# The order of seven outer products in a fast matrix multiplication, and where two weight sums are made

## The chip, the cores and the metric

The kernel runs on one core of a Trainium2 chip. A core has a matrix engine (TensorE, PE in the profile), a vector engine (VectorE, DVE), an activation engine (ScalarE, ACT), a general engine (GpSimd, POOL) and a queue that mostly issues transfers (SyncE, SP). Each works through its own queue in order; semaphores tie the queues together. The metric is the device time of one execution in microseconds (us).

## The reference

The input is four batches of eight heads with 768 rows of 64 numbers. First comes routed attention, then a feed-forward block:

```python
mask = q_assign[:, :, :, None] == k_assign[:, :, None, :]   # nearest of 16 centroids
scores = np.where(mask, scale * np.matmul(q, k.transpose(0, 1, 3, 2)), -1e9)
attn_out = np.matmul(softmax(scores), v)
x = attn_out.transpose(0, 2, 1, 3).reshape(3072, 512)
h = x @ w_in                                  # w_in: 512 x 2048
g = h * (1.0 / (1.0 + np.exp(-1.702 * h)))    # quick Gelu
out = g @ w_out                               # w_out: 2048 x 512
```

All of it is in 32-bit floating point. The feed-forward block is done batch by batch, 768 rows at a time.

## The kernel before

The first part (to 346 us of the profiled span) is attention for all four batches, and the change does not touch it. Then come, for each batch b = 0 to 3, a first layer (72 us) and a second layer (64 us).

**First layer.** It multiplies with seven products of half-size blocks instead of eight (the Winograd form of Strassen's method). A loop over eight columns f makes seven products each on PE (first7, matmuls at L840). VectorE adds them up from PSUM (add, L831), ScalarE copies one and applies the Gelu (L845, L850), and the result lies in the tile G as four blocks. GpSimd makes the sums of w_in for the column after the next (sums_w, 128x256 operations at L593). VectorE follows with after7, which prepares operands of the second layer: G's signs, and from column 4 on one slice per column of the operands of the first outer product (tiles Y[11], E[0], E[1], E[2]).

**Second layer.** It applies the same method twice, so that 49 quarter-size products are made. The outer level has seven outer products, in the order of ORDER; k counts them, and i is the number of the product in the method. second49(k) makes one of them: seven inner products of four matmuls each (L890), in the order 1, 2, 6, 5, 7, 3, 4, accumulated in three PSUM banks x, z, v out of a pool of six. Inner products 1, 2 and 3 read G itself; 6, 5, 7 and 4 read sums of G (t2, t1, t3, t4; sums_t, 128x768 operations on VectorE); 6, 5 and 3 need sums of the weights from the tile W[k] (name Wz, two buffers), and the others read the weights. ScalarE copies from PSUM (L900 to L925), VectorE adds, and the outer product is left in a tile y of 128x768. For i = 1 the tile is Y[22] itself. Then the finished y is added into the quarters Y[11], Y[12], Y[21], Y[22] of the output that need it, on GpSimd (L593, Y<-y,Y), in the last batch for two of the products on VectorE. Product i = 4 comes last and is added into Y[21] piece by piece.

Between these, extra(at) puts other work of VectorE at three places of each outer product: the sums sums_t for the next outer product, sums_G (four operations that turn a block of G in place into the operand of a later outer product), the transposes of a finished quarter with its stores (store, L945 and L949), and the sums of x for the next batch.

**The weight sums.** In batch 0 alone they are made from w_out: three 128x512 operations on GpSimd per outer product (keep_w), into parts of Y[12], Y[21] and Y[22], each then stored to kept_w in main memory (L775). All seven sets are made in columns 3 to 7 of the first layer of batch 0, before which VectorE turns signs in w_out and its sums (turn_w). All batches load them back, three transfers per outer product (load_sums, L782), two outer products ahead.

**The end.** In the last batch the quarter Y[11] is stored from the fifth outer product on, the others in the last one (tail). Stores of the last quarter are cut into pieces and alternate between the queues of SyncE and ScalarE; the others are four transfers each on SyncE. A transfer waits for the one that was issued eight places before it.

Of the kernel before, what the change touches and what calls it, by code (L numbers as in the profile page):

```python
# [38 lines left out]
def fast(  # L39
# [26 lines left out]
    nc = tc.nc  # L66
# [676 lines left out]
                      (Sz(1, f), Sz(2, f), "+", Bz(0, 0, f)),  # L743
                      (Sz(4, f), Bz(1, 0, f), "-", Sz(2, f))))

    ORDER = (1, 7, 3, 2, 6, 5, 4)

    def W_of(i):

# [12 lines left out]
        a = W_of(i)  # L762
        sums(nc.vector, ((a(0, 1), a(0, 0), "-", a(0, 1)),))

    def keep_w(k):

        a = W_of(ORDER[k])
        s2, s1, s4 = (Y[n].rearrange("p a t -> p (a t)")[
            :, 0:FQ * P].rearrange("p (f n) -> p f n", n=P)
            for n in (12, 21, 22))  # L770
        for i, (o, x, op, z) in enumerate((
                (s2, a(1, 1), "-", a(0, 1)), (s1, s2, "+", a(0, 0)),
                (s4, a(1, 0), "-", s2))):
            sums(nc.gpsimd, ((o, x, op, z),))
            nc.sync.dma_start(out=kept_w[k, i], in_=o)  # L775

    W = {}

    def load_sums(k):
        W[k] = ws.tile([P, 3, FQ, P], FP32, name="Wz")  # L780
        for i in range(3):
            nc.sync.dma_start(out=W[k][:, i], in_=kept_w[k, i])  # L782

# [7 lines left out]
    def tile_x(i):  # L791
        return T_of[i].rearrange("p c (q t) -> p (c q) t", t=QT)

    def tile_y(n):
        return Y[n].rearrange("p m (q t) -> p (m q) t", t=QT)

    def temps(k):

        return dict(zip((3, 2, 1, 4), (
            (tile_y(11), E[0], E[1], E[2]),  # L800
            (tile_y(12), tile_x(2), tile_x(3), tile_x(4)),
            (tile_y(11), E[0], E[1], E[2]),
            (tile_x(2), tile_x(3), tile_x(4), E[0]),
            (E[1], E[2], tile_x(4), E[0]),
            (G_of(5)(0, 1), tile_x(2), E[1], E[2]),
            (G_of(4)(0, 1), E[0], E[1], E[2]))[k]))

    def sums_t(k, fs=slice(0, FQ)):
# [67 lines left out]
    def second49(k, extra, last):  # L876

        i = ORDER[k]
        a, g, t, w = W_of(i), G_of(i), temps(k), W.pop(k)
        A = {1: a(0, 0), 2: a(1, 0), 3: w[:, 2], 4: a(1, 1), 5: w[:, 1],  # L880
             6: w[:, 0], 7: a(0, 1)}
        M = {1: g(0, 0), 2: g(1, 0), 3: g(1, 1), 4: t[4], 5: t[1], 6: t[2],
             7: t[3]}

        def bank_b():
            return ps_b.tile([P, 512], FP32, name="b")[:, 0:QT]

        def product(ps, n, start):
            for f in range(FQ):
                nc.tensor.matmul(out=ps, lhsT=A[n][:, f], rhs=M[n][:, f],  # L890
                                 start=start and f == 0,
                                 stop=(f == FQ - 1), skip_group_check=True)

        y = Y[22] if i == 1 else ep.tile([P, 2, HALF], FP32, name="y")
        y11, y12, y21, y22 = (y[:, m, q * QT:(q + 1) * QT]
                              for m in range(2) for q in range(2))
        p5 = ep.tile([P, QT], FP32, name="p5")
        x = bank_b()
        product(x, 1, True)
        nc.scalar.copy(y11, x)  # L900
        z = bank_b()
        product(z, 2, True)
        add(y11, z, y11)
        extra(0)
        product(x, 6, False)
        nc.scalar.copy(y12, x)
        v = bank_b()
        product(v, 5, True)
        nc.scalar.copy(p5, v)
        product(x, 7, False)  # L910
        nc.scalar.copy(y22, x)
        add(y22, y22, p5)
        extra(1)
        product(v, 3, False)
        add(y12, v, y12)
        if i == 4:
            c = Y[21]
            add(c[:, 0], y[:, 0], c[:, 0])
            add(c[:, 1, QT:], y22, c[:, 1, QT:])
            extra(2)  # L920
        product(x, 4, False)
        if i == 4:
            add(c[:, 1, 0:QT], x, c[:, 1, 0:QT])
            return
        nc.scalar.copy(y21, x)  # L925
        extra(2)
        pool = nc.vector if last and i in (6, 5) else nc.gpsimd
        sums(pool, {1: (), 7: ((Y[21], y, "+", Y[22]),),
                    3: ((Y[12], y, "+", Y[22]),),
                    2: ((Y[11], y, "+", Y[22]),),  # L930
                    6: ((Y[12], y, "+", Y[12]), (Y[21], y, "+", Y[21])),
                    5: ((Y[12], y, "+", Y[12]), (Y[22], y, "+", Y[21]))}[i])

    def store(b, n, m=slice(0, 2), q=slice(0, 2), queues=(nc.sync,)):

        h, t = divmod(n, 10)
        h, t = h - 1, t - 1
        o = {11: T_of[3], 12: E[0], 22: E[1], 21: E[2]} if b < B - 1 else {
            11: T_of[3], 12: T_of[3], 22: T_of[4], 21: T_of[2]}
        o = o[n].rearrange("p a t -> p (a t)").rearrange(  # L940
            "p (j m i) -> p j m i", m=2, i=SQ)
        at, to = q.start * QT, q.stop * QT
        o = o[:, at // SQ:to // SQ]
        for one in range(m.start, m.stop):
            nc.vector.transpose(out=o[:, :, one], in_=Y[n][:, one, at:to])  # L945
        rows = out[b * S + t * HALF + at:b * S + t * HALF + to]
        for r in range(P // SQ):
            col = r * P + (2 * h + m.start) * SQ
            queues[r % len(queues)].dma_start(  # L949
                out=rows[:, col:col + (m.stop - m.start) * SQ].rearrange(  # L950
                    "(j t) i -> t j i", t=SQ),
                in_=o[r * SQ:(r + 1) * SQ, :, m].rearrange(
                    "t j m i -> t j (m i)"))
# [26 lines left out]
    for b in range(B):  # L980
        for f in range(FB):
            first7(b, f, *XT)
            sums_w(b * FB + f + 2)
            if f:
                after7(f - 1)
            do(pend, 1)
            if b == 0 and f < 3:
                for n in range(3 * f, min(3 * f + 3, FB)):
                    sums_z((nc.gpsimd, nc.vector, nc.vector)[n % 3], n)
            if b == 0 and f in (3, 4):  # L990
                for i in ORDER[0:4] if f == 3 else ORDER[4:]:
                    turn_w(i)
            if b == 0 and f >= 3:
                for k in {3: (0,), 4: (1, 2), 5: (3,), 6: (4, 5),
                          7: (6,)}[f]:
                    keep_w(k)
                if 5 <= f < 7:
                    load_sums(f - 5)
        after7(FB - 1)
        if b < B - 1:  # L1000
            for h in range(2):
                for hp in range(HP):
                    x = xT_of[b + 1, h, hp] = xp.tile([P, HALF], FP32,
                                                      name="x")
                    nc.sync.dma_start(out=x, in_=kept[b, h, hp])
            made = sums_x(b + 1)
        else:
            made = iter(())

        def stores(b, *todo, **how):  # L1010
            for n in todo:
                store(b, n, **how)
                yield

        both = dict(queues=(nc.sync, nc.scalar))

        def tail():
            for n in (12, 22):
                store(b, n)
                yield  # L1020
            store(b, 21, slice(0, 1), slice(0, 1), **both)
            store(b, 21, q=slice(1, 2), **both)
            yield

        def chain(*todo):
            for steps in todo:
                yield from steps

        def sums_of_x():
            for XT[:] in made:  # L1030
                yield

        x_steps = sums_of_x()
        final = b == B - 1

        for k in range(7):
            nxt = sums_t(k + 1) if k < 6 else iter(())
            more = {1: sums_G(6), 3: sums_G(5),
                    4: chain(sums_G(4), stores(b, 11)), 5: x_steps,
                    6: tail() if final else x_steps}.get(k, iter(()))  # L1040
            if b == B - 1 and k < 2:
                test(k)
            if (b, k) == (B - 1, 6):
                is_bad = nc.values_load(bad[0:1, 0:1], min_val=0, max_val=1)

            def extra(at):
                do(nxt, (2, 1, 1)[at])
                do(more, ((1, 1, 1) if final else (0, 4, 4))[at] if k == 6
                   else (0, 2, 2 + (k == 4))[at])

            second49(k, extra, final)
            if k < 5:
                load_sums(k + 2)
            elif b < B - 1:
                load_sums(k - 5)
        pend = () if final else stores(b, 12, 22, 21)
        if final:
            store(b, 21, slice(1, 2), slice(0, 1), **both)
# [439 lines left out]
```

## Time and profile before

| | us |
|---|---|
| median of three runs (920.73 to 921.88) | 921.24 |
| the profiled execution's own time | 914.16 |
| its span, first to last instruction | 912.4 |
| first layer of batch 0 | 346.6 to 418.9 |
| second layer of batch 0 | 418.9 to 491.7 |
| second layers of batches 1, 2, 3 | 564.0 to 628.0, 700.0 to 764.0, 836.4 to 900.5 |
| after the last matmul | 900.5 to 912.4 |

Busy shares of the span are PE 97%, VectorE 78%, GpSimd 53% and ScalarE 40%. PE is the engine whose idle time counts. A line of the page's slices gives the busy tenths of 40 equal parts of the span. A line of the waits names who waited, for whom, and then microseconds in total, times, and the longest. A line of the timeline gives start, length, engine, line of the code, operation, output and input tiles and shapes, the number of instructions taken together, and in brackets the idle time ahead of it. A line of the windows gives the stretch, its length, the busy time of the five engines, the granted clock, the share of the transfer engines and GB/s.

### The profile page before, as it was taken

To read this page: it belongs to the slowest core of one execution; us is meant where nothing else is said; L and a number is where in the kernel's file an instruction comes from. 1 tells how busy PE (TensorE), PEld (TensorE's weight loads), DVE (VectorE), ACT (ScalarE), POOL (GpSimd) and SP (SyncE) were. 2 spreads that over 40 slices of the span, in tenths; PEclk is the share of its full clock that TensorE was granted. 3 is DMA by queue.
4 is the path that set the end of the run, shared out by engine and by line. 5 is a ranking of instruction groups with operands and counts; after the bars stand their busy time and mean duration, and the time that the engine had idled before them with its cause. 6 is when DMAs were issued, how large, how long until landed. Compare 5 with 4: busy or idle time off the path is not lost.

```text
span 912.4 us, 17739 instructions
## 1 busy us (share of the span) xinstructions
PE 888.9 (97%) x6712; PEld 580.8 (64%) x6712; DVE 712.0 (78%) x1170; ACT 363.2 (40%) x816; POOL 481.1 (53%) x465
## 2 busy tenths in 40 slices
PE   8999999999999999997999999999999999999994
PEld 3444444444444445555998556998557997557994
DVE  4999999998899996998788556788556787556794
ACT  3767767776667773221111232112232112232110
POOL 5899899989999898696134121133121133220110
PEclk9999999999999999998999999999999999999998
DMA  9475556666574210037214202213202313200314
GB/s 184 118 125 102 101 118 144 143 128 136 127 135 111 84 43 18 9 129 243 84 56 122 52 1 70 84 57 120 52 1 70 97 50 115 52 1 1 104 46 97
DMA packets 179261, 80.55 MB, mean 88 GB/s; under 512 B 155368, under 2 KB 161632, under 8 KB 179168
## 3 DMA queue, kind: packets, MB, share of 16 engines
q1 hardware_dynamic: 177776, 79.11, 35.7%
q8 instruction: 55, 0.90, 0.4%
q10 hardware_dynamic: 1392, 0.23, 0.2%
q14 instruction: 38, 0.31, 0.1%
HBM read 62.61 MB, written 16.70 MB: 87 GB/s over the span
## 4 chain that ended last, share of the span: by engine, by line
PE 82%; DVE 5%; POOL 4%; DMA 3%; issue 2%; SPq 2%; ACT 2%; ACTq 0%; DVEq 0%; POOLq 0%
PE b L840 28%; PE b L890 28%; PE s L467 11%; PE o L532 9%; POOL Y L593 3%; PE m L549 2%; PE s L490 2%; ACT A L498 1%; DMA raw<-in_moe_w_out_dram 1%; SPq L418 1%; PE m L343 1%; DMA raw<-in_moe_w_in_dram 1%; POOL W L593 1%; DMA line<-row 1%; DVE x L570 1%
## 5 line engine op out<-in xcount | busy, mean ns | idle before, releaser
L516 POOL TENSOR_TENSOR sum<-sum,A 128x384 f32<-128x384 f32 x252 | 264.0, 1082 | 35.3 <-ACT A L498 22.1
L831 DVE TENSOR_TENSOR G<-b,G 128x384 f32<-128x384 f32 x224 | 123.1, 557 | 100.8 <-PE b L840 90.7
L498 ACT ACTIVATE A<-s 128x768 f32<-128x768 f32 x192 | 144.7, 804 | 94.0 <-PE s L490 73.8
L593 POOL TENSOR_TENSOR Y<-y,Y 128x768 f32<-128x768 f32 x24 | 59.4, 2483 | 186.8 <-DVE y L831 162.9
L467 PE MATMUL s<-T,T 64*64 64x384 f32 x1536 | 144.6, 491 | 2.6 <-ACT A L498 0.9
L845 ACT ACTIVATE G<-G 128x384 f32<-128x384 f32 x128 | 66.3, 523 | 198.1 <-DVE G L831 196.8
L532 PE MATMUL o<-A,inv 64*64 64x384 f32 x1536 | 141.5, 483 | 0.0
L593 POOL TENSOR_TENSOR W<-w_in 128x256 f32<-128x256 f32 x32 | 23.5, 735 | 164.5 <-PE b L840 164.2
L467 PEld LDWEIGHTS s<-T,T 64*64 64x64 f32 x1536 | 52.3, 132 | 78.6 <-ACT A L498 51.5
L840 PE MATMUL b<-x,W 128*128 128x384 f32 x256 | 93.0, 486 | 0.0
L840 PE MATMUL b<-Tx,w_in 128*128 128x384 f32 x256 | 93.0, 486 | 0.0
L840 PE MATMUL b<-x,w_in 128*128 128x384 f32 x256 | 88.5, 486 | 0.0
L593 DVE TENSOR_TENSOR G<-G 128x768 f32<-128x768 f32 (+1 forms) x88 | 84.3, 980 | 0.0
L532 PEld LDWEIGHTS o<-A,inv 64*64 64x64 f32 x1536 | 59.4, 133 | 37.6 <-issue 32.6
L840 PEld LDWEIGHTS b<-x,W 128*128 128x128 f32 x256 | 48.6, 190 | 33.9
L840 PEld LDWEIGHTS b<-Tx,w_in 128*128 128x128 f32 x256 | 48.6, 190 | 33.9
L840 PEld LDWEIGHTS b<-x,w_in 128*128 128x128 f32 x256 | 48.5, 190 | 33.5 <-issue 0.6
L890 PE MATMUL b<-E,Wz 128*128 128x192 f32 x256 | 47.7, 337 | 6.4 <-ACT Y L900 6.4
L890 PE MATMUL b<-G,w_out 128*128 128x192 f32 x288 | 50.3, 326 | 0.1
L890 PEld LDWEIGHTS b<-E,Wz 128*128 128x128 f32 x256 | 44.0, 197 | 7.5 <-ACT Y L900 6.7
L890 PEld LDWEIGHTS b<-G,w_out 128*128 128x128 f32 x288 | 47.4, 190 | 1.5 <-ACT G L845 0.4
L840 PE MATMUL b<-Tx,W 128*128 128x384 f32 x128 | 46.5, 486 | 0.0
(166 smaller groups left out, 1380.3 us busy)
## 6 DMA issues: line engine op xcount, KB each, us to landing
Wz<-kept_w SPq DMA_DIRECT2D x84, 256.0 KB
raw<-in_moe_w_in_dram SPq DMA_DIRECT2D x16, 512.0 KB
raw<-in_moe_w_out_dram SPq DMA_DIRECT2D x16, 512.0 KB
inv<-in_v_dram SPq DMA_DIRECT2D x16, 384.0 KB
in<-in_q_dram SPq DMA_DIRECT2D x60, 96.0 KB
in<-in_k_dram SPq DMA_DIRECT2D x60, 96.0 KB
kept_w<-Y SPq DMA_DIRECT2D x21, 256.0 KB
kept<-x SPq DMA_DIRECT2D x24, 192.0 KB
```

The lines of the kernel that those rows point to most:

```text
L343: nc.tensor.matmul(out=ps[r:r + SQ, w * NJ * SQ:(w + 1) * NJ * SQ] .rearrange("p (j t) -> p j t", t=SQ), lhsT=cT[:, p % HP].rearrange("p a ...
L467: nc.tensor.matmul(out=ps[c:c + D, a, 0:HALF], lhsT=T[p, 1][rows, kt * P + c:kt * P + c + D], rhs=T[p, 0][rows, h * HALF:(h + 1) * HALF], ...
L490: nc.tensor.matmul(out=s_of[u][c:c + D, a, :], lhsT=rows_of[1, p % 2][rows, kt * P + c:kt * P + c + D], rhs=rows_of[0, p % 2][rows, h * HA ...
L498: nc.scalar.activation(out=A_of[u], in_=s_of.pop(u), func=AF.Exp, scale=SCALE)
L516: nc.gpsimd.tensor_tensor(out=sum_of[g][:, a], in0=(A_of[u - 1] if kt == 1 else sum_of[g])[:, a], in1=A_of[u][:, a], op=ALU.add)
L532: nc.tensor.matmul(out=o_of[g][a * D:(a + 1) * D, r, 0:HALF], lhsT=v_in[p][rows, a, kt, :], rhs=A[rows, a, :], start=(kt == 0), stop=(kt = ...
L549: nc.tensor.matmul(out=ps[a * D:(a + 1) * D, 0:HALF], lhsT=twos, rhs=sm[:, a, :], start=(i == 0), stop=(i == len(parts) - 1))
L593: engine.tensor_tensor(out=o, in0=a, in1=b, op=(ALU.add if op == "+" else ALU.subtract))
L831: nc.vector.tensor_tensor(out=o, in0=p, in1=a, op=ALU.add)
L840: nc.tensor.matmul(out=ps[:, 0:HALF], lhsT=a[:, c], rhs=x(c), start=(c == 0), stop=(c == 1))
L845: nc.scalar.activation(out=g, in_=g, func=AF.Gelu_apprx_sigmoid, scale=2.0)
L890: nc.tensor.matmul(out=ps, lhsT=A[n][:, f], rhs=M[n][:, f], start=start and f == 0, stop=(f == FQ - 1), skip_group_check=True)
```

## The change

Four things change together.

1. ORDER becomes 1, 2, 3, 6, 5, 7, 4. With it go the quarters that each outer product is added into: quarter 11 is complete after the second outer product (before: after the fourth), 12 and 22 after the fifth and the sixth, 21 after the seventh. Over a batch there are eight such additions ahead of the last product, not seven.
2. The tiles for the operands t follow the new order, sums_G(5) and sums_G(4) move one outer product earlier, and the four operations of sums_G(5) stand together at the end of the third.
3. keep_w takes its three output tiles as an argument. Sets 0 to 4 are made in columns 3 to 6 of the first layer. Sets 5 and 6 are made in the second layer of batch 0, at the end of the fourth and the fifth outer product, directly into the W tile that uses them, and stored from there; batch 0 does not load these two.
4. The stores of quarter 11 come one place earlier, in the fifth outer product's second gap, and use another tile; in the last batch those of quarter 12 move from the seventh to the sixth outer product, and quarter 22 is stored at the first gap of the seventh.

```diff
-    ORDER = (1, 7, 3, 2, 6, 5, 4)
+    ORDER = (1, 2, 3, 6, 5, 7, 4)
...
-    def keep_w(k):
+    def keep_w(k, o):
         a = W_of(ORDER[k])
-        s2, s1, s4 = (Y[n].rearrange("p a t -> p (a t)")[
-            :, 0:FQ * P].rearrange("p (f n) -> p f n", n=P)
-            for n in (12, 21, 22))
+        s2, s1, s4 = o
...
-    def load_sums(k):
+    def load_sums(k, made=False):
         W[k] = ws.tile([P, 3, FQ, P], FP32, name="Wz")
+        if made:
+            keep_w(k, [W[k][:, i] for i in range(3)])
+            return
...
             (tile_y(12), tile_x(2), tile_x(3), tile_x(4)),
-            (tile_y(11), E[0], E[1], E[2]),
+            (tile_y(21), E[0], E[1], E[2]),
             (tile_x(2), tile_x(3), tile_x(4), E[0]),
-            (E[1], E[2], tile_x(4), E[0]),
-            (G_of(5)(0, 1), tile_x(2), E[1], E[2]),
+            (G_of(5)(0, 1), E[1], E[2], E[0]),
+            (G_of(7)(0, 1), tile_x(3), E[1], E[2]),
...
-        pool = nc.vector if last and i in (6, 5) else nc.gpsimd
-        sums(pool, {1: (), 7: ((Y[21], y, "+", Y[22]),),
+        pool = nc.vector if last and i in (5, 7) else nc.gpsimd
+        sums(pool, {1: (),
+                    2: ((Y[11], y, "+", Y[22]),),
                     3: ((Y[12], y, "+", Y[22]),),
-                    2: ((Y[11], y, "+", Y[22]),),
-                    6: ((Y[12], y, "+", Y[12]), (Y[21], y, "+", Y[21])),
-                    5: ((Y[12], y, "+", Y[12]), (Y[22], y, "+", Y[21]))}[i])
+                    6: ((Y[12], y, "+", Y[12]), (Y[21], y, "+", Y[22])),
+                    5: ((Y[12], y, "+", Y[12]), (Y[22], y, "+", Y[21])),
+                    7: ((Y[22], y, "+", Y[22]), (Y[21], y, "+", Y[21]))}[i])
...
-                for k in {3: (0,), 4: (1, 2), 5: (3,), 6: (4, 5),
-                          7: (6,)}[f]:
-                    keep_w(k)
+                for k in {3: (0,), 4: (1, 2), 5: (3,), 6: (4,), 7: ()}[f]:
+                    keep_w(k, spare_y())
...
-            for n in (12, 22):
-                store(b, n)
-                yield
+            store(b, 22)
+            yield
...
-            more = {1: sums_G(6), 3: sums_G(5),
-                    4: chain(sums_G(4), stores(b, 11)), 5: x_steps,
+            more = {1: sums_G(6), 2: sums_G(5), 3: sums_G(4),
+                    4: stores(b, 11), 5: stores(b, 12) if final else x_steps,
...
-                do(more, ((1, 1, 1) if final else (0, 4, 4))[at] if k == 6
-                   else (0, 2, 2 + (k == 4))[at])
+                do(more, ((1, 0, 1) if final else (0, 4, 4))[at] if k == 6
+                   else (0, 0, 4)[at] if k == 2 else (0, 2, 2)[at])
...
-                load_sums(k + 2)
+                load_sums(k + 2, b == 0 and k > 2)
```

spare_y() is a new helper that returns the parts of Y[12], Y[21] and Y[22] which keep_w named itself before.

More of the change, by code (lines that the diff above doesn't have):

```diff
@@ L775, in keep_w, with spare_y @@
             nc.sync.dma_start(out=kept_w[k, i], in_=o)
+    def spare_y():
+        return [Y[n].rearrange("p a t -> p (a t)")[:, 0:FQ * P].rearrange(
+            "p (f n) -> p f n", n=P) for n in (12, 21, 22)]
     W = {}
-    def load_sums(k):
+    def load_sums(k, made=False):
         W[k] = ws.tile([P, 3, FQ, P], FP32, name="Wz")
+        if made:
+            keep_w(k, [W[k][:, i] for i in range(3)])
+            return
         for i in range(3):
@@ L937, in store @@
         h, t = h - 1, t - 1
-        o = {11: T_of[3], 12: E[0], 22: E[1], 21: E[2]} if b < B - 1 else {
-            11: T_of[3], 12: T_of[3], 22: T_of[4], 21: T_of[2]}
+        o = {11: T_of[4], 12: E[0], 22: E[1], 21: E[2]} if b < B - 1 else {
+            11: T_of[4], 12: T_of[4], 22: T_of[2], 21: T_of[3]}
         o = o[n].rearrange("p a t -> p (a t)").rearrange(
```

## The prediction

> **What bounds the kernel now.** I read the slices first: PE is busy in nearly every slice, at the full clock in all but one, so only what makes PE wait, or what follows its last matmul, can move the time. Then the waits of the mixture-of-experts half: PE's queue stops there once.
>
> ```profile
> PE   8999999999999999997999999999999999999994
> PEclk9999999999999999998999999999999999999998
> ...
> PE b L890 <- ACT Y L900: 6.4, 1, 6.4
> ...
> ACT Y L900 <- DMA kept_w<-Y: 6.7, 1, 6.7
> ```
>
> The chain in order of time (start, length in us) shows where: in batch 0, GpSimd makes weight sums without a pause, the last is stored from Y[22], and only then may ScalarE copy the second layer's first result into Y[22].
>
> ```profile
> 421.89 1.34 POOL Y L593
> ...
> 423.30 2.61 POOL Y L593 x2
> ...
> 425.93 1.99 DMA kept_w<-Y
> ...
> 428.39 3.89 PE b L890 x11
> ```
>
> The timeline gives the same sum on VectorE beside GpSimd and alone (1.30 and 0.36 us), and VectorE held up while GpSimd adds a product into a quarter (3.44 for two that take 1.82 elsewhere).
>
> ```profile
> 422.14 1.30 DVE L593 TENSOR_TENSOR E<-Y,G 128x192 f32<-128x192 f32 x1
> 426.88 0.36 DVE L593 TENSOR_TENSOR E<-Y,G 128x192 f32<-128x192 f32 x1
> ...
> 447.49 2.30 POOL L593 TENSOR_TENSOR Y<-y,Y 128x768 f32<-128x768 f32 x1 [21.59 <-DVE y L831]
> 448.04 3.44 DVE L593 TENSOR_TENSOR G<-G 128x768 f32<-128x768 f32 x2
> ```
>
> The end: PE stops at 900.5. SyncE issues the stores of three quarters in one row until 907.56, and waits among them for earlier stores to land; packets move until about 908.
>
> ```profile
> 896.29 11.27 SPq L949 DMA_DIRECT2D out_dram<-Tx  x14
> SPq L949 <- DMA out_dram<-Tx: 2.0, 2, 1.8
> 901.73 0.38 DVE L945 STREAM_TRANSPOSE Tx<-Y 128x192 f32<-128x192 f32 x1
> 905.00:907.00 2.00, 0.00 (x0) 0.00 (x0) 0.00 (x0) 0.00 (x0) 0.00 (x0) 0.50 0.62 108
> 907.00:909.00 2.00, 0.00 (x0) 0.00 (x0) 0.00 (x0) 0.00 (x0) 0.00 (x0) 0.50 0.32 57
> ```
>
> **What the Trainium skill says.** "SBUF — State Buffer", Who interferes with whom: a Vector instruction with two SBUF inputs and a GpSimd instruction that reads SBUF exclude each other for a whole instruction; one SBUF input doesn't contend. The trace agrees: the pair above loses 1.6 us, about the 1.65 that the GpSimd operation needs by itself, while the adds from PSUM (L831) take 0.55 with GpSimd busy or not. "DMA: Bandwidth & Descriptors", Issuing engines are not separate DMA queues: stores of both queues share 16 engines, a second queue saves only issue time; the tail moves 102 to 111 GB/s however they are issued, so there bytes count too.
>
> **The change, part by part.**
>
> *(a) Two weight sums leave the first layer of batch 0.* GpSimd loses six 128x512 operations before the second layer, 1.27 to 1.4 us each. In before, sums five, six and seven run 411.20-415.54, 415.54-419.34, 421.85-425.93. Now the fifth is the last; its store lands near 417.6, before ScalarE can want Y[22] (420.5). That wait goes. What is late next is VectorE. With GpSimd free from 415.5 its sum at 414.37 (2.65 for two) gets about 1.0 shorter; its seven adds end near 419.8 instead of 420.8; then the tensor sums of the last two columns run uncontended: 0.55+0.35+0.36+0.63 and 0.55+0.35+0.36. The last slice of E0 is there at 422.9. PE finishes its first two products at 421.6 and needs that slice for its twelfth matmul, 1.0 later: a wait of 0.3 to 0.4. Before: 6.38, and 0.35 for a late Gelu. **Gain 6.3**; both ends: 5.4 if PE waits for the whole of E0, 6.7 if for nothing.
>
> *(b) They come back in the fifth and sixth outer products.* There GpSimd already has two quarter sums per product (the new order makes eight in a batch where before had seven; 1.65 us of the port each), and VectorE four tensor sums t3, t2, t1, t4 of 0.95. In the second, third and fourth product VectorE also has four G sums of 0.9 each; those of sums_G(5) now come in one lump at the end of the third. A weight operation holds the port about 1.2 us (1.27 in a row of them). I lay the rows one behind the other, GpSimd taking the port at VectorE's next boundary (in four of five places in before it did). Zero is the start of batch 0's fourth product; the next start at 9.1, 18.3, 27.4 (64.0/7 = 9.14 each). A product that starts at S needs t2 and its first weight sum at S+2.6, t1 and the second at S+3.9.
>  - VectorE was done with product three at 0.7 (455.87 against 455.17). One quarter sum and the lump: 0.7+1.65+3.6 = 5.9.
>  - Product four (makes t for five): add, t3, t2 to 8.1; add, t1 to 9.25; two G sums, add, t4 to 12.2; then quarter sum (to 13.85), G sum (14.75), quarter sum (16.4), G sum (17.3) in turn. Product five needs t2 at 11.7 and has it at 8.1.
>  - Product five (makes t for six): weight operation to 18.5, t3 19.4, weight operation 20.6, t2 21.5, weight operation 22.7, t1 23.6, transposes of quarter 11, add, t4 to 25.9. Product six needs t2 at 20.9: 0.6 late; t1 then at 22.8: 0.8 late. PE waits 1.4.
>  - Product six (makes t for seven): quarter sum to 27.55, t3 28.5, quarter sum 30.15, t2 31.1, weight operation 32.3, t1 33.2, weight operation 34.4. Product seven, now at 28.8, needs the first weight sum at 31.4: 0.9 late; the second at 33.6: 0.8 late. PE waits 1.7.
> Sum 3.1; with VectorE winning each race instead I get 0.2 and 4.2. **I take a loss of 3.4.** Ends: 0 if the two engines overlap better, 7 if both orders' worst come together. The six stores from Wz wait on SyncE for GpSimd; behind them stand the store of quarter 11 and the next batch's Wz loads, which nobody needs before its second layer some 72 us on. The stores are as many as before, two triples of loads fewer: nothing. So is the new place of the sign turns of the weights (seven on VectorE either way, one 1.75 us operation changing columns; PE doesn't wait for VectorE anywhere in that stage of before, and at most 1.75 would show if it did).
>
> *(c) The new order in batches 1 to 3.* Same matmuls. Without (b)'s operations the layout gives t2 of product six at 18.9 to 19.5 against 20.9, of product seven 27.6 against 30.0: no wait, 1.4 spare at the least. If that cover failed, each us would count three times. Work on x goes in under product six and seven as before. **Zero.**
>
> *(d) The tail.* Quarter 12 is complete one product earlier; its transposes come under product six and its four stores are issued near 893 to 895. Quarter 22's transposes come 1.2 earlier, at the start of product seven (VectorE is free at 896.3, transposes to 897.3), stores 897.4-899.4. The last quarter is made as before (899.82 to 902.11, set by PE). SyncE then has 6 stores, not the rest of 14: two at 901.0, two near 901.5, two from 902.1, at about 0.5 each plus a wait for a store eight places earlier: done by 904. Bytes: from 901 on before moved 2x(102+111+108+57) = 756 KB; now about 393 KB (384x256x4), at 108 GB/s 3.6 us from 901.3: 905.0 against 908.1. **Gain 3.1**; ends 0 (small stores set the end regardless) and 4.
>
> Sum 6.3 - 3.4 + 0 + 3.1 = 6.0. The profiled execution took 914.16 with a span of 912.4 and should become 908.2 and 906.4. The runs' median, 921.24, lies 7.1 above it; I take the 6.0 from the median: **915.2**.
>
> **Rivals.** *R1, the returned sums stay hidden*: no wait in product six and seven; for it, PE never waited in the second layers of before though VectorE lagged by 2.5 us; against it, the port's work there. Gain 9.4: 911.8. *R2, the tail gives nothing*: the last quarter's own stores (128-byte and 256-byte rows, twelve of them) take the time that was freed. For it, they were the last anyway; against it, twice the bytes moved before. 6.3-3.4: 918.3. *R3, the wait is replaced more fully*: late weight sums cost 6.5 instead of 3.4. For it, the other order of races; gain 2.9: 918.3. *R4, slower*: VectorE falls behind in every batch, because sums_G(5) comes as a lump just before product four's operands, so product six waits for t2 in all four. Its price is four times the lateness; (c) has 1.4 to 2 us spare, and it decides once each batch waits over 1.5 us (4x1.5 = 6.0), so when VectorE is over 3 us later than laid out. At 2.5 each: 925.2. *R5, the change doesn't do what it says*: Y[22] still held at the switch; the fifth sum's store has 3 us to spare, so I give it no chance of its own.
>
> **How the numbers follow.** Forecast 0.53 (its own range 913.3 to 917), R1 0.17, R2 0.12, R3 0.10, R4 0.04, and 0.04 for pieces that cancel to within 0.2% (1.8 us, about what a measurement of this kernel can tell from no change). Holding eight in ten needs R1 and most of R2 and R3: 911.4 to 918.8. Faster 0.92, same 0.04, slower 0.04.
>
> **What would show it.** (a) no wait of PE for L900's copy in batch 0, a wait under 1 us for E0 instead. (b) PE waits of 1 to 4 us in all in product six and seven of batch 0 alone, released by GpSimd's Wz or a tensor sum. (c) no PE wait in later second layers. (d) SyncE's last store issued near 904, its longest row of stores ending there. Wrong if PE waits in batches 1 to 3, if GpSimd's Wz sums come over 3 us late, or if packets still move at 908.

## The result and the profile after

The changed kernel takes 910.64 us (median of four runs, 909.60 to 910.91); the kernel before took 920.99 beside it (919.62 to 921.88, four runs). The ratio is 0.9887, with an interval of 0.9870 to 0.9904. The time fell by 10.35 us; the prediction said 6.0, and 910.64 lies under its range of 911.4 to 918.8. The direction was right, the size was not. The profiled execution took 910.43 with a span of 908.5. That is only 3.7 below the *profiled* execution of before (914.16), and it is a first hint at where the error lies.

The slices of the page, after: PE has no slice at 7 any more, and the one slice with a clock of 8 near the middle has gone.

```profile
PE   8999999999999999999999999999999999999994
PEclk9999999999999999999999999999999999999998
```

PE's waits in the feed-forward half, after (who, for whom, total, times, longest): the 6.4 us for the copy into Y[22] are gone, and three short waits have come.

```profile
PE b L845 <- DVE Tx L593: 1.5, 1, 1.5
PE b L895 <- DVE E L593: 1.4, 2, 0.7
```

The chain in order of time, after (start, length): where the chain of before went to GpSimd, its store and back, this one stays on PE across the switch at 419.4.

```profile
394.69 24.83 PE b L845 x77
419.52 3.58 PE b L895 x22
```

The timeline of batch 0, after, shows what the returned weight sums do. GpSimd's three operations hold the port that VectorE's two-input sums need; VectorE's operands come late for product six (470.09) and seven (480.41), and the sums of x, two of which take 4.24 us beside GpSimd's quarter sums, make the next first layer wait too (488.63).

```profile
465.05 1.87 POOL L593 TENSOR_TENSOR Wz<-Wz,w_out 128x512 f32<-128x512 f32 x1
470.09 1.54 PE L895 MATMUL b<-E,Wz 128*128 128x192 f32 x8 [0.67 <-DVE E L593]
...
480.41 1.54 PE L895 MATMUL b<-E,Wz 128*128 128x192 f32 x8 [0.68 <-DVE E L593]
...
483.33 4.24 DVE L593 TENSOR_TENSOR x<-x 128x384 f32<-128x384 f32 x2
...
488.63 1.56 PE L845 MATMUL b<-Tx,W 128*128 128x384 f32 x4 [1.49 <-DVE Tx L593]
```

Where the time went is read best by stage: the start of each layer's first matmul in the timeline, in three executions. The last two are from the experiments below; each is a usual one of its kernel.

| us | before, the profile shown first (914.16) | before, profiled later (920.28) | after (910.12) |
|---|---|---|---|
| start of batch 0's first layer | 346.57 | 347.06 | 346.80 |
| second layer, batch 0 | 72.65 | 74.87 | 66.34 |
| first layer, batch 1 | 72.24 | 72.24 | 74.00 |
| second layer, batch 1 | 63.96 | 65.67 | 63.96 |
| second layer, batch 2 | 63.96 | 65.63 | 63.96 |
| second layer, batch 3 | 64.24 | 64.23 | 64.23 |
| after the last matmul | 11.91 | 11.95 | 12.12 |
| span | 912.4 | 918.5 | 908.2 |

The other first layers take 72.24 to 72.35 everywhere. Two things stand out. The execution of 920.28 is longer than the one on which the prediction was built, in the second layers of batches 0, 1 and 2, by 2.2, 1.7 and 1.7. And the time after the last matmul, from which 3.1 us were to come, has not moved.

### The profile page after: what moved, and what is told of

The parts are those of the page before. It is cut to its first block, busy times and chain, and to the rows that moved or that the text cites. A ratio compares the mean times of both kernels' runs of the same rounds, so it can differ in the third digit from the quotient of the medians.

```text
span 908.5 us, 17741 instructions
## 1 busy us (share of the span) xinstructions
PE 888.4 (98%) x6712; PEld 577.7 (64%) x6712; DVE 728.6 (80%) x1170; ACT 363.3 (40%) x816; POOL 492.1 (54%) x469
## 4 chain that ended last, share of the span: by engine, by line
PE 81%; DVE 9%; DMA 3%; issue 2%; SPq 2%; ACT 2%; POOL 0%; DVEq 0%; ACTq 0%
PE b L845 32%; PE b L895 23%; PE s L467 11%; PE o L532 9%; PE m L549 3%; PE s L490 2%; DVE G L593 2%; DMA raw<-in_moe_w_out_dram 2%; DVE E L593 1%; ACT A L498 1%; SPq L418 1%; DVE Tx L593 1%; PE m L343 1%; DMA line<-row 1%; DVE x L570 1%
## 5 line engine op out<-in xcount | busy, mean ns | idle before, releaser
L593 POOL TENSOR_TENSOR Y<-y,Y 128x768 f32<-128x768 f32 x28 | 67.4, 2422 | 175.0 <-DVE y L836 151.0
L593 DVE TENSOR_TENSOR G<-G 128x768 f32<-128x768 f32 (+1 forms) x92 | 104.1, 1156 | 0.0
L895 PE MATMUL b<-G,w_out 128*128 128x192 f32 x320 | 55.9, 326 | 0.0
L895 PEld LDWEIGHTS b<-G,w_out 128*128 128x128 f32 x320 | 52.7, 190 | 1.1
L895 PE MATMUL b<-E,Wz 128*128 128x192 f32 x288 | 51.5, 328 | 1.4 <-DVE E L593 1.4
L895 PEld LDWEIGHTS b<-E,Wz 128*128 128x128 f32 x288 | 47.1, 190 | 3.4 <-POOL Wz L593 1.3
```

The lines of the kernel that those rows point to most:

```text
L593: engine.tensor_tensor(out=o, in0=a, in1=b, op=(ALU.add if op == "+" else ALU.subtract))
L895: nc.tensor.matmul(out=ps, lhsT=A[n][:, f], rhs=M[n][:, f], start=start and f == 0, stop=(f == FQ - 1), skip_group_check=True)
```

## The experiments

The theories at the start: the missing gain was time that PE loses to its clock after the long wait (called C), or time lost elsewhere in a usual execution of before (E). The first four kernels ran in one series, beside 71 runs of before (median 917.46, 914.25 to 921.49). Their expectations give times reckoned from 921 us, so that what counts in them is the gain, not the time itself.

**The kernel before, once more.** No edit.

> The kernel before, unchanged, to see where an execution of 921 us differs from the profiled one of 914.16. Theory C (clock): the 6.4 us in which TensorE waits in batch 0 lower its granted clock for a stretch afterwards (0.5 for 6.8 us in the profile of before, which cost 2.1 us), and in most executions that stretch is longer, so the 7 us lie between the second outer product of batch 0 and the first layer of batch 1, with a mean clock of 0.98 or so. Theory E (elsewhere): the 7 us lie in the attention part or at the end, and the mean clock is 0.99 as in the profile.

It took 917.3 (913.36 to 919.93, 20 runs), ratio 0.999 [0.9976, 1.0005]; its profiled execution took 919.02, so that it shows what the first profile did not. Its attention, first layers and tail equal those of the first profile within 0.3 us. Its second layers take 74.31, 65.64 and 65.70, then 64.23: 1.66, 1.68 and 1.74 more in the first three. PE's waits say for whom:

```profile
PE b L890 <- ACT Y L900: 6.4, 1, 6.4
PE b L890 <- DMA Wz<-kept_w: 3.0, 2, 1.5
PE b L890 <- DVE Tx L593: 1.5, 1, 1.5
```

The last of these, too, ends at a matmul that reads Wz (762.19, in batch 2). So the time lies elsewhere, as E said, but in neither of the two places that E named. Here is the fifth product of batch 1 in the timeline, first in the profile of 914.16:

```profile
611.31 6.59 POOL L593 TENSOR_TENSOR Y<-y,Y 128x768 f32<-128x768 f32 x2 [7.12 <-DVE y L831]
611.92 1.82 DVE L593 TENSOR_TENSOR G<-G 128x768 f32<-128x768 f32 x2
...
613.66 1.03 DVE L945 STREAM_TRANSPOSE Tx<-Y 128x384 f32<-128x384 f32 x2
...
614.72 1.91 SPq L949 DMA_DIRECT2D out_dram<-Tx  x4
...
616.73 11.22 SPq L782 DMA_DIRECT2D Wz<-kept_w  x9
...
621.27 2.76 PE L890 MATMUL b<-E,Wz 128*128 128x192 f32 x16
```

and the same place in the execution of 919.02:

```profile
612.69 4.85 POOL L593 TENSOR_TENSOR Y<-y,Y 128x768 f32<-128x768 f32 x2 [7.13 <-DVE y L831]
613.30 5.05 DVE L593 TENSOR_TENSOR G<-G 128x768 f32<-128x768 f32 x2
...
618.28 1.02 DVE L945 STREAM_TRANSPOSE Tx<-Y 128x384 f32<-128x384 f32 x2
...
619.33 1.91 SPq L949 DMA_DIRECT2D out_dram<-Tx  x4
...
621.34 9.64 SPq L782 DMA_DIRECT2D Wz<-kept_w  x9
...
624.24 2.84 PE L890 MATMUL b<-E,Wz 128*128 128x192 f32 x16 [1.43 <-DMA Wz<-kept_w]
```

GpSimd's two quarter sums and VectorE's two sums of G start 0.61 us apart in both. In the first, VectorE gets the port (1.82 for two) and GpSimd takes 6.59; in the second GpSimd gets it (4.85) and VectorE takes 5.05. Behind VectorE's sums stand the transposes of quarter 11, behind those on SyncE the quarter's stores, and behind the stores, in the same queue, the load of the last weight sums W[6] (the first three of the nine transfers). Issued at 616.73 it has landed before PE asks for it at 621.27; issued at 621.34 it makes PE wait. This became theory L: a load that stands behind a store which it has nothing to do with, and a race that decides in each of three batches whether it costs 1.7 us.

**PE kept busy during the wait.** Thirty matmuls whose result nobody reads, issued while PE waits at the switch:

```diff
+        if i == 1 and first:
+            warm = bank()
+            for _ in range(30):
+                nc.tensor.matmul(
+                    out=warm, lhsT=ident_h,
+                    rhs=ident_h[:, None, :].broadcast_to((P, 4, P)),
+                    start=True, stop=True)
```

> Before, with thirty 128x512 bfloat16 matmuls into an unused bank put between the first two and the third inner product of batch 0's second layer, so that TensorE works while it waits. The wait for the copy into Y[22] stays. Theory C: the clock stays at 1.0, and the time falls by the whole dip, 2 us against a 914 us execution and 7 to 9 against a 921 us one: 912 to 914. Theory E: 2 us at most, 919; and if the matmuls only come on top, 923.

It took 916.57 (912.07 to 918.87), ratio 0.9976 [0.9960, 0.9991], which is 0.9 less than before by the medians and 2.2 by the ratio. The timeline of PE after the wait, with these matmuls:

```profile
421.87 6.64 PE L907 MATMUL m<-ident_h 128*128 128x512 bf16 x30
428.44 2.87 PE L890 MATMUL b<-E,Wz 128*128 128x192 f32 x16
```

and in the first profile of before:

```profile
428.39 4.85 PE L890 MATMUL b<-E,Wz 128*128 128x192 f32 x16 [6.38 <-ACT Y L900]
```

The same sixteen matmuls take 2.87 and 4.85. C holds, but for 2.0 us, not 7: the wait costs that much more than its length.

**The weight sums alone.** The order, the quarters and the stores of before, with only part 3 of the change: sets 5 and 6 made in the second layer.

```diff
-                for k in {3: (0,), 4: (1, 2), 5: (3,), 6: (4, 5),
-                          7: (6,)}[f]:
-                    keep_w(k)
+                for k in {3: (0,), 4: (1, 2), 5: (3,), 6: (4,), 7: ()}[f]:
+                    keep_w(k, spare_y())
...
-                load_sums(k + 2)
+                load_sums(k + 2, b == 0 and k > 2)
```

> The old order of the outer products; only sums six and seven are made in the second layer of batch 0. My prediction's step (a) says 6.3 us gained and (b) about 3 lost: 918. Theory C adds the dip of the clock to (a): 6.4 + 2 to 9 - 3, so 909 to 914. If the new order was what gained, no change: 920.

It took 913.94 (910.65 to 916.23), ratio 0.9965 [0.9953, 0.9977]: 3.5 less than before, about the 3 of the prediction's (a) and (b) and not the 7 to 12 of theory C.

**The order alone** is the complement: ORDER, quarters, operand tiles and stores of the changed kernel, all seven sets in the first layer.

```diff
-                for k in {3: (0,), 4: (1, 2), 5: (3,), 6: (4,), 7: ()}[f]:
+                for k in {3: (0,), 4: (1, 2), 5: (3,), 6: (4, 5),
+                          7: (6,)}[f]:
                     keep_w(k, spare_y())
...
-                load_sums(k + 2, b == 0 and k > 2)
+                load_sums(k + 2)
```

> The new order, stores and tiles of the changed kernel, but all seven weight sums made in the first layer. My prediction's step (d) says 3.1 us gained at the end: 918. Theory C with the tail of the changed kernel's trace (last store issued 7.5 us after TensorE's end, 7.1 before) says nothing gained: 920 to 922.

It took 915.15 (913.93 to 918.05), ratio 0.9969 [0.9957, 0.9982]: 2.3 less than before by the medians, 2.8 by the ratio. PE's waits, weight sums alone:

```profile
PE b L895 <- DVE E L593: 3.0, 2, 2.5
PE b L895 <- DMA Wz<-kept_w: 1.5, 1, 1.5
PE b L895 <- DVE Tx L593: 1.5, 1, 1.5
```

and the order alone:

```profile
PE b L895 <- ACT Y L905: 6.4, 1, 6.4
```

Each half removes what the other leaves. The late sums take the stop at the switch away and keep the late load (second layers of batches 1 and 2: 65.67 and 65.73); the new order takes the late load away (63.96 in both) and keeps the stop. The prediction costed the order at zero outside the end of the kernel; its 3.1 were to come from that end, which has not moved (12.33 after the last matmul). So the gain of the order alone has about the expected size by chance: it comes from another place. The changed kernel didn't run in this series, so the two gains can't be added up against its 10.35.

In the old order, PE's stop in product seven of batch 0 is longer than in the new one, 2.5 us, and the clock falls to half for 3.41 us from 480.08 on, although PE is at work again. Eight matmuls then take 2.74, where they take 1.46 elsewhere.

```profile
478.83 1.69 PE L895 MATMUL b<-E,Wz 128*128 128x192 f32 x8 [2.52 <-DVE E L593]
481.04 2.74 PE L895 MATMUL b<-E,Wz 128*128 128x192 f32 x8 [0.52 <-DVE E L593]
...
480.00:484.00 4.00, 3.48 (x14) 3.06 (x13) 4.00 (x7) 0.49 (x2) 1.75 (x1) 0.57 0.79 287
```

**The load moved, nothing else.** In the kernel before, the loads of W[6] are put ahead of quarter 11's stores on SyncE, first in all batches:

```diff
-                    4: chain(sums_G(4), stores(b, 11)), 5: x_steps,
+                    4: sums_G(4), 5: x_steps,
...
                 load_sums(k + 2)
+                if k == 4:
+                    store(b, 11)
```

> The kernel before, with one thing moved: the three loads of the last product's kept weight sums (the sixth Wz of a batch) are issued on SyncE ahead of quarter 11's four stores, not behind them. Theory L (the load stands behind the stores, and a race between VectorE and GpSimd in the fifth product decides in each batch whether it comes 1.65 us late): PE waits for no DMA of Wz in any of the four second layers, each later one takes 64 to 64.3 us, the stop of 6.4 us at the switch stays; median 914.3, and the executions lie within about 2 us of each other instead of 7. Theory O (the scatter comes from elsewhere, the late load is only its sign): median within 1 us of the kernel before on this chip, scatter as before.

It took 916.85 (916.69 to 917.42, six runs), before beside it 920.28 (919.75 to 923.31, eleven runs), ratio 0.9960 [0.9948, 0.9972]. No wait for Wz was left, and the six times lie within 0.7 us (before: 3.6); but the level is 2.5 above the 914.3 that was expected. Of these, 1.6 come after the last matmul (13.52, against 11.91), where the last batch's stores had changed their order too, and 0.7 lie in the first layers of batches 1 to 3 (72.40, 72.63 and 72.36, in place of 72.24). So it was done again with the last batch left alone (the stores of quarter 11 stay in the chain where b is the last batch):

> The kernel before, with the sixth Wz loads of the first three batches ahead of quarter 11's stores, and the last batch left as it was, so that the end of the kernel keeps its form (the run with all four batches moved had no wait for Wz and a narrow scatter, but 1.6 us more after PE's last matmul). Theory L: no wait for Wz; tail 11.9 to 12.3 again; span 912.4 to 913.6, time 914.3 to 915.5, scatter under 2 us; the stop of 6.4 us and the half clock after it stay. Theory O (the cost comes from elsewhere): no lower than 916.5.

It took 915.7 (914.82 to 917.17, five runs), before beside it 920.0 (917.68 to 921.01, nine runs), ratio 0.9957 [0.9941, 0.9974]: 0.2 above theory L's range and 0.8 below the least that theory O allowed. Its scatter was 2.4 us, not under 2, and its tail (13.06) and span (914.7) lie above L's ranges too. In the stages L holds: no wait for Wz, and the second layers of batches 0 to 2 take 72.98, 63.96 and 63.96, together 5.3 less than in the execution of 920.28. Its timeline of batch 1:

```profile
609.21 2.14 SPq L782 DMA_DIRECT2D Wz<-kept_w  x3
...
612.05 4.85 POOL L593 TENSOR_TENSOR Y<-y,Y 128x768 f32<-128x768 f32 x2 [7.12 <-DVE y L831]
...
618.69 1.91 SPq L949 DMA_DIRECT2D out_dram<-Tx  x4
...
622.02 2.76 PE L890 MATMUL b<-E,Wz 128*128 128x192 f32 x16
```

This settles the mechanism: GpSimd won the race here, as in the execution of 919.02, and the stores are as late (6.64 after GpSimd's start in both), and yet PE doesn't wait, since the load left 9.5 us before them. VectorE's lateness without the load costs little: the next first layers take 72.38, 72.61 and 72.31, 0.6 more in all, against 1.7 in each batch with it. For the 1.1 us more after the last matmul the trace has a place: SyncE's second store after PE's end goes out 4.50 us after it (2.55 in the first profile), once a piece of ScalarE's has landed that has the same semaphore (how these tie the two queues is shown below). SyncE's waits at the end, where before had 2.0:

```profile
SPq L949 <- DMA out_dram<-Tx: 3.8, 2, 2.0
```

**The kernel before, in the third series.** No edit; one profiled execution.

> The kernel before, unaltered, profiled on this chip, to see in the stages what an execution of about 920 us consists of. Theory L: each of the second layers of the first three batches that is 1.5 to 1.8 us longer than in the profile of 914.16 us has a wait of PE for a Wz load; three of them give 919, two 917.4; the rest of an execution (first layers, tail, attention) agrees within 1 us with the profile of before.

It took 920.28, and its stages stand in the table above. PE's waits:

```profile
PE b L890 <- DVE Tx L593: 1.6, 1, 1.6
PE b L890 <- DVE y L831: 1.5, 1, 1.5
PE b L890 <- DMA Wz<-kept_w: 1.4, 1, 1.4
```

All three end at a matmul that reads Wz, one in each of batches 0 to 2: GpSimd won the race in all three. PE starts on W[6] 3.02, 2.95 and 2.91 us after the load is issued (3.00, 2.90 and 2.98 in the execution of 919.02), whichever engine the records name as the releaser. The 6.1 us of span over the first profile are 2.2, 1.7 and 1.7 in the three batches and 0.5 before the first.

**The changed kernel in the second series.** No edit.

> The changed kernel unaltered, for the comparison on this chip. Theory L: 910.5 within 1, scatter under 2 us, 3.5 to 4 below the loads moved ahead (half-clock stretch 2, tail 0.5 worse, switch 6.4 less its own waits of 2.8). If theory L is wrong, the difference to the loads moved ahead is that to the kernel before, 6 to 7 us.

It took 910.16 (909.82 to 910.94), ratio 0.9888 [0.9872, 0.9904]: the same gain. Its profiled execution, 910.12, is the one in the table. Against the loads moved ahead in all batches it is 6.7 lower. That is the size that was named as the sign against theory L; but the terms named for L make 5.1, not 3.5 to 4 (2 + 6.4 - 2.8 - 0.5), and the stages show where the 6.7 lie: 4.9 in batch 0's second layer and the first layer after it, 1.4 after the last matmul, 0.5 in the later first layers, and none in the second layers of batches 1 to 3, where a late load would show.

**The end: one queue for the last quarter's pieces.** In the changed kernel:

```diff
-        both = dict(queues=(nc.sync, nc.scalar))
+        both = dict(queues=(nc.sync,))
```

> The changed kernel, with the last quarter's six pieces issued on SyncE alone, two by two in the order of before, ScalarE issuing none. Theory S (quarter 22's third and fourth store waited 5 us because they share their completion signals with ScalarE's pieces that are issued later): those two stores are issued right after the first two, before 894; the stores after them wait less than 2 us for earlier ones, the last is issued 6 to 7 us after PE's end rather than 7.5, and the time is 0.5 to 1.5 lower. Theory B (the end is set by the issue time of the pieces or by their bytes): the last store and the time stay within 0.5, or get worse by up to 2, since twelve issues of 0.5 us stand on one queue.

First what it is to change. SyncE's waits at the end of the changed kernel (from 880 on), and its and ScalarE's stores in the timeline:

```profile
SPq L955 <- DMA out_dram<-Tx: 6.1, 2, 5.3
```

```profile
887.94 15.88 SPq L955 DMA_DIRECT2D out_dram<-Tx  x14
...
896.59 3.88 ACTq L955 DMA_DIRECT2D out_dram<-Tx  x6
```

Each transfer signals one of eight semaphores and waits until its previous user has landed. The trace of the changed kernel has these, with the time of issue and the semaphore's number:

```
SyncE    quarter 22: 891.99 (100), 892.35 (103), 898.14 (104), 898.61 (105)
ScalarE  quarter 21: 896.59 (104), 896.99 (105), 897.54 (106), 897.97 (109), 898.52 (101), 900.02 (102)
SyncE    quarter 21: 900.82 (106), 901.18 (109), 901.90 (100), 902.40 (101), 902.94 (102), 903.38 (103)
```

ScalarE's first piece (104) lands at 898.12, and quarter 22's third store, which has the same semaphore, goes out at 898.14. So quarter 22's third and fourth store wait for ScalarE's pieces, which come later in time, but earlier in the order in which the semaphores were given out. With one queue they go out at 891.75 and 892.27, and SyncE has no wait for a landing there: S is right on the mechanism. The time is 909.41 (908.84 to 910.48), ratio to before 0.9882 [0.9866, 0.9898], 0.75 below the changed kernel; the intervals overlap. The end itself has hardly moved: the last issue ends 7.2 us after PE's end (7.5 and 7.4 in the two profiles of the changed kernel; S had said 6 to 7), and the time after PE's end is 11.77 against 12.12. Of this profile's 1.3 us of shorter span, 1.05 lie in batch 0's second layer, where one of the two stops didn't come; nothing there was edited. So little is to be had that way, and for the end B is nearer: whether the issue of twelve pieces, at about 0.5 each, or their bytes set it now, no run here separates.

**The end: ScalarE for the last piece alone.** With one queue and one late set (below), the four stores after PE's last matmul go to ScalarE.

```diff
-            store(b, 21, slice(1, 2), slice(0, 1), **both)
+            store(b, 21, slice(1, 2), slice(0, 1),
+                  queues=(nc.scalar,))
```

> The kernel with only the seventh weight sums late, and the last quarter's third piece (the four stores that follow PE's last matmul) issued on ScalarE, the first two pieces on SyncE. If the serial issue of twelve stores on SyncE (0.5 us each, the last 7.2 us after PE's end) sets the end, the last store is issued about 5 us after PE's end, packets end 1.5 to 2 us earlier, and the time is 906.3 to 907.3. If the bytes or the last landing set it, the time stays within 0.5 of 908.3.

It took 910.51 (910.23 to 910.88, four runs), 2.2 more than its parent in the second series, not 1.5 less. SyncE's waits at the end:

```profile
SPq L955 <- DMA out_dram<-Tx: 7.3, 1, 7.3
```

ScalarE issues its four from 897.01 on, and SyncE its eight, ready earlier, only from 900.52: the first of them shares its semaphore with ScalarE's first. It is the trouble of the changed kernel, made larger. That the bytes or the number of stores would have allowed more is not shown.

**One late set.** One queue as above, and only the seventh set made in the second layer:

```diff
-                for k in {3: (0,), 4: (1, 2), 5: (3,), 6: (4,), 7: ()}[f]:
+                for k in {3: (0,), 4: (1, 2), 5: (3,), 6: (4, 5), 7: ()}[f]:
...
-                load_sums(k + 2, b == 0 and k > 2)
+                load_sums(k + 2, b == 0 and k > 3)
```

> The kernel with one queue for the last quarter's pieces, and only the seventh weight sums made in the second layer of the first batch; the sixth are made in the first layer again. Theory of the port (each weight sum that comes back costs what VectorE loses to it): the two stops of 0.7 in product six go, those in product seven stay within 0.7 to 1.7; at the switch the sixth sums end near 420 and their store holds the copy into Y[22] for 0 to 3 us. Sum of waits in batch 0 between 1 and 4.5 us, time from 1.5 below to 1.5 above the kernel with one queue. Rival (the seventh alone causes all the stops): no gain, and the switch's wait on top.

It took 908.3 (907.56 to 909.19), ratio to before 0.9863 [0.9847, 0.9879]: the lowest of all, 1.9 below the changed kernel beside it. PE's waits are 1.2 in batch 0, for a slice of E at 424.89, and 1.0 in the next first layer. Their sum, 2.2, lies in the range of the theory of the port; but the stop in product seven, which was to stay, is gone as well. And the two stages together, second layer and the next first, take 139.14, against 139.29 in the run with one queue and two late sets, so the two profiles don't show the gain over that kernel, and the run doesn't decide between the theory and its rival.

## Why the prediction was wrong

**The base.** "I take the 6.0 from the median": this is the step that failed most, together with the "Zero" of (c). The 7.1 us between the profiled execution and the median were carried along as an offset that no change would touch. Some 5 of them (1.66, 1.68, 1.74 in one later profile) were W[6]'s load, late in three batches; it was on time in all three in the execution that was profiled. The changed kernel removes them: its second layers of batches 1 and 2 take 63.96, and its times lie within 1.3 us.

**(b), on stores and loads, and (c).** "Behind them stand the store of quarter 11 and the next batch's Wz loads, which nobody needs" looked at one side of the queue only: what stands *behind* the returned stores. What stands behind quarter 11's own store is W[6], needed 4.5 us after its issue in the first profile (616.73, 621.27), and it was 1.6 us from being late (landed near 619.7). (c) costed the new place of that store at zero. In the changed kernel store 11 goes out after a shorter run of sums, and W[6] is loaded 6.6 us before PE asks for it, where 2.9 to 3.0 are enough. In batch 1:

```profile
608.37 2.10 SPq L955 DMA_DIRECT2D out_dram<-Tx  x4
...
610.58 13.23 SPq L787 DMA_DIRECT2D Wz<-kept_w  x9
...
617.14 2.76 PE L895 MATMUL b<-E,Wz 128*128 128x192 f32 x16
```

No load is late in any profile of the changed kernel. The prediction counted races "in four of five places" for GpSimd; the fifth place, where VectorE won in the first profile, was this one.

**(a)** was right on the wait: the 6.38 are gone, and for E0's last slice the weight loads waited 0.32 at 423.12 (released by DVE E), PE itself 0.03. It left out that the clock was halved for 6.83 us, 4.06 of them after the wait, which was in the slices as the one 8. Sixteen matmuls took 4.85, in place of 2.76 to 2.87: 2.0 us mis-sized. The Trainium skill has it ("TensorE: Matmul & The Clock Gate", Part 1: the clock halves after an idle window of about 3.4 us and comes back after a busy one); the trace agrees, with half clock from 3.6 us after PE's stop to 4.1 after its restart. A stop shorter than that window can do it too: the 2.5 us in the run with the weight sums alone brought 3.41 us of half clock.

**(b), the returned sums**, was right in size: PE waits 1.4 in products six and seven and 1.5 in the next first layer, 2.85 against 3.1 laid out and 3.4 taken; by the length of the stages they cost 3.8 (below). "SBUF — State Buffer", Who interferes with whom, has the two engines exclude each other for a whole instruction, and the trace agrees: a weight sum that takes 1.27 alone took 1.9 to 2.0 in five of six. (The 1.65 that the prediction gave a quarter sum "by itself" is an estimate: 447.49 + 2.30 less 448.12, where VectorE's sum ends, makes 1.67; the shortest such sum in that trace takes 1.81.) The place was half wrong: each product stopped 0.7, not 1.4 and 1.7, and the rest went to sums of x under product seven, which (b) did not lay out.

**(d)** fell. The last store was to be issued 3.5 us after PE's end (904 against 900.5); its issue ended 7.5 after it (7.1 before). "A wait for a store eight places earlier" was read as eight places in time. The semaphores were given out in another order than that of issue, so that two stores of quarter 22 waited 5.3 us for ScalarE's pieces, and their bytes still moved at the end. With that wait taken away the end came 0.35 earlier, not 3.1. So R2 was right that the end gives nothing. Its reason, the last quarter's own stores, is left standing by the run with one queue but not isolated; the wait for ScalarE's pieces was not in it.

**The sum.** The profile of 910.43 against the first profile, by stage: the stop at the switch and its slow clock, 8.4 together, are gone, but batch 0's second layer and the first layer after it are only 4.6 shorter (66.33 for 72.65, and 74.00 for 72.24). So the returned sums cost 3.8 there. The end is 0.3 longer and attention 0.4, which leaves 3.8 where 6.0 had been laid out. The medians fell by 10.35: the late load adds 5.1, if the usual run is late in three batches as the two later profiles of before are (no other run of before shows its batches); 1.4 remain, of which the execution of 920.28 has 0.5 ahead of the first layer and 0.6 in batch 0, and which no run isolates. So the forecast was 2.2 too high for the profiles and 4.4 too low for the medians; that it missed its range by 0.8 alone is errors of opposite sign. Of the rivals, R2's view of the end came true, but not its time of 918.3; R1, R3 and R4 did not.

## What to carry to other kernels

If the one profiled execution lies well below the runs' median, the difference may be work or waits that the profile doesn't show, as 5 of 7 us were here: take a second profile, or look for places where a race decides and a transfer lands with a slack smaller than what the race moves. When a store is given a new place, look at what is issued behind it on its queue before and after, whoever asked for it. And an idle stretch of a matrix engine is to be priced at its length plus the slow clock after it; here stops of 1.5 us brought none, and stops of 2.5 and 6.4 us did.

## What the runs showed of the hardware that was not expected

- Two pairs of sums, on VectorE and GpSimd, that start 0.61 us apart in both executions met the shared port in either order (6.59 and 1.82, or 4.85 and 5.05). Where PE was kept busy at the switch, the load was late in two of the three batches and on time in one, so that it is not settled once for an execution.
- A wait of 6.4 us costs PE 2.0 more through its clock; it is the idle time itself that brings it about, since matmuls without use took it away. In the run with the weight sums alone a stop of 2.5 us was enough for 3.41 us at half clock.
- A transfer of one queue can wait for a later one of another queue, where both take turns on eight semaphores: 5.3 us here, 7.3 when the pieces were dealt out differently.
